# Retention in halves of 64 tokens, all its small products in 64x64 quarters of the array, the decay factor on the token rows

## The chip, the cores and the metric

The kernel runs on one core of one Trainium2 chip. The metric is device time in microseconds (us) of that core. Three timed runs of the kernel before gave 444.48, 444.49 and 444.55; the median is 444.49.

A core has a matrix engine (PE in the profile; PEld is its loading of weights), a vector engine (DVE), an engine for activations and copies (ACT), a general engine that also issues gathers and scatters (POOL), and SP, which in this kernel issues nearly all loads. DMA engines move data between the chip's main memory and on-chip memory. A matrix product reads both operands from on-chip memory and writes a *bank* of an accumulator memory, of which there are eight; DVE and ACT copy from there.

## What is computed

```python
state = gamma * state + einsum('bhd,bhe->bhde', k[:, :, t], v[:, :, t])   # for t in 768 tokens
y[:, :, t] = scale * einsum('bhd,bhde->bhe', q[:, :, t], state)
...
x = y, as 3072 rows of 512 (4 batches x 768 tokens; 8 heads x 64)
logits = x @ w_gate + modality_bias[modality_id]
e = argmax(logits);  gate = softmax(logits)[e]
out = gate * (relu(x @ w1[e]) @ w2[e])             # 8 experts, w1 512x1024, w2 1024x512
```

All of it is float32. The first two lines are *retention* (attention with a decaying state), the rest a mixture of experts in which each token goes to one expert.

## The kernel before

**Retention** goes through 24 chunks of 128 tokens (`NN`; six to each of four batches). The heads stand in four groups `g` of two heads `j`, so that a group's features fill 128 partitions. For a chunk, PE makes four kinds of products, each eight of them, all in float32:

- `scores` (L190): keys by queries of the chunk, 64 features deep, 128 by 128 tokens out, one bank for each `j`. DVE multiplies them by a triangular mask into `a` (L195).
- `state` (L251): keys by the decayed values `vd`, added in one bank `st` over a batch's six chunks. ACT copies it to `s` (L256) for the next chunk. The last chunk of a batch needs none.
- `heads_out`: the earlier chunks' part, `s` by queries (L211, absent in a batch's first chunk), and the chunk's own, `vd` by `a` (L217), added into two banks. DVE multiplies the sum by a decay factor for each feature and token into `yT` (L223, four instructions of 128x128).
- `tokens_out` (L234): `yT` is turned to token rows `x` and multiplied by the gate weights in the same four products, 136 columns wide. ACT copies the rows to `xs` (L238), and DVE adds up the gate logits (L242).

POOL makes `vd`, values times a decay factor (`decay_v`, L827). Queries and keys by feature (`kq`, 512 KB a chunk) and keys and values by token (`kv`, 512 KB) are loaded by SP. For every three chunks a *group* is routed: DVE finds expert and gate, PE makes ranks (`rk`, L299 to L306), POOL scatters the rows `xs` to `x_dram`, sorted by expert. After some groups (`EVENTS`) a list of full slots of 256 rows of one expert is made, by small products `pc`, `pk` and `pt` and DVE operations that end in `lst` (L512).

**Experts** are done in 12 jobs of 256 rows. `start_job` lets SP read expert and rows from a list; SP then loads the expert's `w1` (`raw1`, four times 512 KB), the rows (`xg`) and `w2` (`raw2`). Each piece of weights is cut into a high and a low part, `hi` by ACT (L596) and `lo` by DVE (L598), and PE makes three products for each exact one: `h_e` (L652) and `o_e` (L667). Rows beyond the jobs go in small units at the end.

**The order** on PE, ACT, DVE and SP is written out by the program: these engines work their instructions off in the order of the calls. Retention is a generator that yields twice for each chunk. First it runs alone (the *dense stage*), until `2 * (DENSE - n)` half steps after the first list has been issued at chunk `n` (`DENSE = 10`). After that, each job of 16 steps takes in five half steps of retention (the *job stage*). SP's loads are one queue: what a chunk or a job needs stands behind what was called earlier. `kv` has three buffers, and four more for chunks 3 to 6; an accumulator bank is handed on when its last reader is done.

## Time and profile before

| what | value |
|---|---|
| median of three runs | 444.49 us |
| the profiled execution's own time | 446.39 us |
| its span, first to last instruction | 444.4 us |
| mean granted PE clock | 0.976 |
| PE busy | 414.1 us, 93% of the span |
| PEld, DVE, ACT, POOL busy | 358.7, 265.5, 185.7, 103.9 us |
| first product of the first job (`h_e`) | 66.2 us |
| last retention product | about 264 us |
| last product of PE | 433.5 us |

The profile is one execution. A row of a group gives the source line, the engine, the operation, what it writes and reads, its shapes and count; then the busy time and the mean of one in ns; then the idle time of the engine before it and what ended it. The chain of waits is the work that ended last, followed back in time. A float32 product of the program shows as two MATMUL records and two LDWEIGHTS records, so that a row "x16" of retention is eight products. A table by stretch of time gives, for each stretch, its length, the busy time and the number of records of each engine, the granted clock of PE (1.00 is full), the share of time that the DMA engines were busy, and GB/s.

### The profile page before, as it was taken

The page shows a single profiled execution, that of the slowest core. Times are in us where ns is not written, and L with a number is a line of the kernel's source. Part 1 is how long each engine was busy: PE and PEld are TensorE (multiplying, and loading weights), DVE is VectorE, ACT ScalarE, POOL GpSimd, SP SyncE. Part 2 cuts the span into 40 slices and gives each one's busy share as a digit, 9 for nine tenths or more (in the row PEclk, how much of TensorE's full clock was granted, in tenths as well). Part 3 has the DMA queues.
Part 4 walks back from the last instruction along what each step waited for, and adds up shares of the span by engine and source line. Part 5 has one row for each costly group of instructions (what it writes and reads, how often), then busy time and mean ns, then how long its engine had stood idle before and what let it go on. Part 6 is the DMA issues. An engine that isn't in the chain of part 4 may idle for free.

```text
span 444.4 us, 9973 instructions
## 1 busy us (share of the span) xinstructions
PE 414.1 (93%) x3619; PEld 358.7 (81%) x3619; DVE 265.5 (60%) x619; ACT 185.7 (42%) x323; POOL 103.9 (23%) x130
## 2 busy tenths in 40 slices
PE   2997898998999999999999999999999999999990
PEld 2886788987988978987987897989789898868860
DVE  1697479846646765695576667855556473725500
ACT  1222143634426334634544453545455655536310
POOL 2225306012401131142112303068410101001010
PEclk9999598999999999999999999999999999999996
DMA  8992697980542758334950405445167579995000
GB/s 279 400 406 104 222 380 274 350 333 28 169 145 96 250 194 324 119 125 154 288 180 26 150 1 175 140 150 215 45 227 280 190 257 337 412 386 195 1 25 19
DMA packets 28722, 89.45 MB, mean 201 GB/s; under 512 B 5310, under 2 KB 5438, under 8 KB 28672
## 3 DMA queue, kind: packets, MB, share of 16 engines
q1 hardware_dynamic: 23200, 74.27, 47.4%
q0 software_dynamic: 5184, 14.10, 8.3%
q8 instruction: 29, 0.48, 0.5%
q10 hardware_dynamic: 288, 0.43, 0.3%
q14 instruction: 21, 0.17, 0.1%
HBM read 91.19 MB, written 17.84 MB: 245 GB/s over the span
## 4 chain that ended last, share of the span: by engine, by line
PE 56%; issue 20%; DVE 8%; DMA 6%; POOL 5%; ACT 2%; SPq 0%; POOLq 0%; ACTq 0%; DVEq 0%
PE h_e L652 17%; PE o_e L667 16%; PE sc L190 6%; PE x L234 5%; PE y L217 5%; PE y L211 3%; POOL x_dram L388 2%; DVE lo_e L598 2%; PE st L251 2%; DMA x_dram<-zer,pad_i 2%; POOL out_dram L680 2%; ACT hi_e L596 2%; DMA kq<-in_qkv_dram 1%; DMA raw<-in_w_dram 1%; PE xp_e L637 1%
## 5 line engine op out<-in xcount | busy, mean ns | idle before, releaser
L598 DVE TENSOR_TENSOR lo_e<-raw,hi_e 128x1024 fp32r<-128x1024 f32 x80 | 98.1, 1226 | 65.4 <-ACT hi_e L596 59.6
L652 PE MATMUL h_e<-xTh,lo_e 128*128 128x256 f32 x320 | 91.3, 285 | 1.7 <-DVE lo_e L598 1.7
L652 PE MATMUL h_e<-xTh,hi_e 128*128 128x256 f32 x320 | 92.8, 290 | 0.0
L652 PE MATMUL h_e<-xTl,hi_e 128*128 128x256 f32 x320 | 91.1, 285 | 0.0
L596 ACT CAST hi_e<-raw 128x1024 fp32r<-128x1024 f32 x80 | 83.4, 1043 | 0.0
L667 PE MATMUL o_e<-hi_e,hTh 128*128 128x512 f32 x160 | 65.8, 411 | 0.0
L652 PEld LDWEIGHTS h_e<-xTh,hi_e 128*128 128x128 f32 x320 | 61.9, 193 | 3.1 <-issue 1.0
L652 PEld LDWEIGHTS h_e<-xTh,lo_e 128*128 128x128 f32 x320 | 62.0, 194 | 2.2 <-DVE lo_e L598 1.9
L667 PE MATMUL o_e<-lo_e,hTh 128*128 128x512 f32 x160 | 62.7, 392 | 0.5 <-DVE lo_e L598 0.5
L667 PE MATMUL o_e<-hi_e,hTl 128*128 128x512 f32 x160 | 62.6, 391 | 0.0
L652 PEld LDWEIGHTS h_e<-xTl,hi_e 128*128 128x128 f32 x320 | 62.0, 194 | 0.0
L605 ACT ACTIVATE hTh<-h_e 128x256 fp32r<-128x256 f32 x80 | 30.7, 383 | 60.4 <-PE h_e L652 56.5
L827 POOL TENSOR_TENSOR vd<-kv,cst 128x512 f32<-128x512 f32 x24 | 25.6, 1068 | 108.0 <-PE y L217 58.6
L195 DVE TENSOR_TENSOR a<-sc,cst 128x512 f32<-128x512 f32 x48 | 30.8, 683 | 24.3 <-PE sc L190 24.3
L680 POOL DMA_INDIRECT out_dram<-o_e,xg_e x20 | 19.9, 994 | 107.9 <-ACT o_e L679 83.9
L606 DVE SCALAR_TENSOR_TENSOR hTl<-h_e,hTh 128x256 fp32r<-128x256 f32 x80 | 33.3, 418 | 16.2 <-ACT hTh L605 14.0
L679 ACT ACTIVATE o_e<-o_e,xg_e 128x512 f32<-128x512 f32 x20 | 13.8, 688 | 67.2 <-issue 35.5
L190 PE MATMUL sc<-kq 64*128 64x128 f32 x384 | 30.6, 304 | 7.9 <-DMA kq<-in_qkv_dram 7.9
L328 POOL DMA_INDIRECT x_dram<-xs,pos x24 | 28.8, 1201 | 33.2 <-DVE key L469 18.4
L667 PEld LDWEIGHTS o_e<-lo_e,hTh 128*128 128x128 f32 x160 | 30.0, 188 | 7.7 <-DVE lo_e L598 1.0
L667 PEld LDWEIGHTS o_e<-hi_e,hTh 128*128 128x128 f32 x160 | 30.1, 188 | 7.5 <-issue 1.4
L667 PEld LDWEIGHTS o_e<-hi_e,hTl 128*128 128x128 f32 x160 | 30.1, 188 | 5.1
(167 smaller groups left out, 604.9 us busy)
## 6 DMA issues: line engine op xcount, KB each, us to landing
raw<-in_w_dram SPq DMA_DIRECT2D x96, 512.0 KB
kv<-in_qkv_dram SPq DMA_DIRECT2D x24, 512.0 KB
kq<-in_qkv_dram SPq DMA_DIRECT2D x23, 512.0 KB
xg_e<-x_dram SPq DMA_DIRECT2D x20, 272.0 KB
wa_u<-in_w_dram SPq DMA_DIRECT2D x8, 512.0 KB
wb_u<-in_w_dram SPq DMA_DIRECT2D x8, 512.0 KB
xg_s<-x_dram SPq DMA_DIRECT2D x4, 272.0 KB
x_dram<-xs,pos POOLq DMA_INDIRECT x24
```

The costliest lines, as they stand in the source:

```text
L190: nc.tensor.matmul(pe[j][:, g * P : (g + 1) * P], kt[r, g], qt[r, g], start=True, stop=True, skip_group_check=True,)
L195: nc.vector.tensor_tensor(a[:, j], pe[j].rearrange("p (h t) -> p h t", t=P), mask.unsqueeze(1).to_broadcast([P, NG, P]), op=ALU.mult,)
L217: nc.tensor.matmul(py[j][g % 2 * D : (g % 2 + 1) * D, g // 2], vd[:, 2 * g + j], a[:, j, g], start=(s is None and g < 2), stop=(g >= 2), s ...
L328: ins = nc.gpsimd.indirect_dma_start(out=x_dram[:, :], out_offset=bass.IndirectOffsetOnAxis(ap=pos[:, i : i + 1], axis=0), in_=xs.rearrang ...
L596: nc.scalar.copy(hi, raws[m][i])
L598: nc.vector.tensor_tensor(lo, raws[m][i], hi.bitcast(F32), op=ALU.subtract)
L605: nc.scalar.activation(hi, src, AF.Relu)
L606: nc.vector.scalar_tensor_tensor(lo, src, 0.0, hi.bitcast(F32), op0=ALU.max, op1=ALU.subtract)
L652: nc.tensor.matmul(ph, s["w1"][f // 2][wi][:, o : o + P], s["xT"][kc // 2][a][:, kc % 2, :], start=(n == 0), stop=(n == 3 * KC - 1),)
L667: nc.tensor.matmul(po, hT[f][a][:, hh * P : (hh + 1) * P], s["w2"][f // 2][wi][:, (f % 2) * DM : (f % 2 + 1) * DM], start=(n == 0), stop=( ...
L680: ins = nc.gpsimd.indirect_dma_start(out=out[:, :], out_offset=bass.IndirectOffsetOnAxis(ap=xg.bitcast(I32)[:, 0, P : P + 1], axis=0), in_ ...
L827: ins = nc.gpsimd.tensor_tensor(vds[n], vv, dec[:, n % NCH].unsqueeze(2).to_broadcast([P, H, D]), op=ALU.mult)
```

## The change

Each chunk is worked in two halves `u` of 64 tokens, and every product of retention but `tokens_out` becomes 64x64x64: it uses a quarter of the 128x128 array, given by the half of the partitions it reads (`low` or `high`) and the half it writes. `scores` within a half, the part between the halves through a state of its own, and so on: 64 quarter products for a chunk, 56 where a chunk is a batch's first or last. `run` issues two of the `low` half, then two of the `high` half, and so on. `quarters(n)` is one stretch of them on PE: scores of chunk n+1, the state after chunk n and after the first half of chunk n+1, the rest of the output of chunk n-1 and most of that of chunk n.

```diff
-DENSE = 10
+DENSE = 12
-ROW = DM // P * (P + NE)
+ROW = DM + 2
+XW = P + 2 * NE
...
+    def keep_state(n, u):
+        s = sts[n, u] = wk.tile([P, NG, D], F32, tag="s", name=f"s{u}_{n}", bufs=3)
+        b = (n - 1 + u) // NCH
+        nc.scalar.copy(s, pst.pop(b) if u and n % NCH == NCH - 1 else pst[b])
+
+    def run(low, high):
+        for i in range(0, max(len(low), len(high)), 2):
+            for out_, l, r, start in low[i : i + 2] + high[i : i + 2]:
+                nc.tensor.matmul(out_, l, r, start=start, stop=True, skip_group_check=True)
+
+    def quarters(n):
+        more = 0 <= n < NN and (n + 1) % NCH
+        ...
+        if n + 1 < NN:
+            low += scores(n + 1, 0)
+        if more:
+            high += grown(n, 1)
+        if n > 0:
+            low += inner(n - 1, 1, 0)
+            high += inner(n - 1, 0, 1)
+        if 0 <= n < NN:
+            low += inner(n, 0, 0, start=True) + outer(n, 0)
+            high += inner(n, 1, 1, start=True) + outer(n, 1)
+        run(low, high)
+        if more:
+            keep_state(n + 1, 0)
+        if n + 1 < NN:
+            run(grown(n + 1, 0), scores(n + 1, 1))
+            keep_state(n + 1, 1)
...
-        for b in range(NG):
-            nc.vector.scalar_tensor_tensor(
-                yT[:, b], py[b // 2][:, b % 2], step[:, n % NCH, b : b + 1], dcq[:, b],
-                op0=ALU.mult, op1=ALU.mult,
-            )
+    def y_out(n):
+        yT = wk.tile([P, NG, P], F32, tag="yT", name=f"yT_{n}")
+        for j in range(2):
+            nc.scalar.copy(yT[:, 2 * j : 2 * j + 2], py[n][j])
...
-            nc.scalar.copy(xs[:, 2 * u : 2 * u + 2], px)
+            gained(lh[:, hs], px[:, :, P:], NE)
+            if u == 0:
+                gained(x, px[:, :, :P], D)
+            else:
+                for i in range(4):
+                    nc.scalar.activation(
+                        x[:, i], px[:, i // 2, rows(i % 2)], AF.Copy,
+                        scale=gain[:, c, 4 * u + i : 4 * u + i + 1],
+                    )
...
-        vds[n] = wk.tile([P, H, D], F32, tag="vd", name=f"vd_{n}", bufs=2)
+        vds[n] = wk.tile([P, H, D], F32, tag="vd", name=f"vd_{n}", bufs=3)
...
+        for n in range(NN + 1):
+            if n > 0:
+                if n > 1:
+                    tokens_out(n - 2, yT)
+                if n > 1 and (n - 1) % GRP == 0:
+                    route((n - 1) // GRP - 1)
+                yield n
+            quarters(n)
+            if n + 1 < NN:
+                masked(n + 1)
+            if n + 2 < NN:
+                decay_v(n + 2)
+            if n > 0:
+                yT = y_out(n - 1)
+            load_kv(n + 7 if n < 3 else n + 3)
+            load_kq(n + 8 if n < 4 else n + 4)
```

`grown` is the state's products (into the bank `st`), `inner` the output within a half and between the halves, `outer` the earlier state's part, `masked` DVE's mask (two instructions of 128x256 in place of 128x512). `gained` multiplies the token rows by the decay factor, on DVE for the gate logits `lh` and for the first half of the row; ACT does the other half in four instructions of 128x64. The gate weights double to 16 columns a group, so that `tokens_out` writes 144 columns. A row of `x_dram` shrinks from 272 KB to 257 KB for 128 rows, the table `decq` (256 KB) is no longer loaded, and the constants grow from 168 to 212 KB and stand behind the first `kq` on ACT's queue. In the small units `w2` is loaded in eight pieces in place of four. All products of retention have line L257, `tokens_out` L313, the state's copy L251, the `yT` copies L302, and the row's scaling on ACT L335.

Three places of the order follow. On PE, the kernel before had these rows shortly ahead of the first `h_e` of job 0 (only `rk` and `pc` stand between; `xp1` are the rows of job 0 turned, `e10` is that job; `kv_10` is chunk 10's, and chunk 11's `kv` was first used inside job 0):

```order
L637 MATMUL xp1_e10_962<-cst_76,xg0_e10_798 128x128
L637 MATMUL xp1_e10_962<-cst_76,xg1_e10_800 128x128
L251 MATMUL st_6_580<-vd_10_868,kv_10_683 64x64 x8
L190 MATMUL sc0_11_990<-kq_11_422 128x128
L190 MATMUL sc1_11_991<-kq_11_422 128x128
```

The change has, also between the first list (`pt1`) and the first `h_e`, the whole of `quarters(10)`; this is where its second `run` begins (`s1_10` is the state inside chunk 10, `sc1_11` the scores of the second half of chunk 11):

```order
L257 MATMUL y0_10_1337<-kq_10_431,s1_10_1284 64x64 x2
L257 MATMUL y1_10_1338<-kq_10_431,s1_10_1284 64x64 x2
L257 MATMUL st_6_767<-vd_11_1289,kv_11_1194 64x64 x2
L257 MATMUL sc1_11_1390<-kq_11_541 64x64 x2
L257 MATMUL st_6_767<-vd_11_1289,kv_11_1194 64x64 x2
```

So `kv_11` and `vd_11` are now needed in the dense stage, and `tokens_out` of chunks 9 and 10, `quarters(11)`, the rows of job 0 turned (`xp`) and `quarters(12)` stand between this and the first `h_e`.

SP's queue of loads has, in the change, this order there; it is that of the kernel before, where line numbers and the size of `xg` differ (`raw10` to `raw13`, the pieces of `w1`, and `xg0` stand ahead of these rows; `ISA` rows are waits):

```order
L705 DMA xg1_e10_1108<-x_dram_75 128x514
L677 ISA
L677 DMA raw20_107<-in_w2_dram 128x1024
L677 ISA
L677 DMA raw21_108<-in_w2_dram 128x1024
L677 ISA
L677 DMA raw22_109<-in_w2_dram 128x1024
L677 ISA
L677 DMA raw23_110<-in_w2_dram 128x1024
L108 DMA kv_11_1194<-in_qkv_dram 128x1024
```

So `kv_11` stands behind the whole first set of weights in both kernels; only what waits for it has moved.

On ACT, a chunk of the dense stage was this before (the state's copy, then the rows):

```order
L256 COPY s_8_816<-st_6_580 128x256
L238 COPY xs_7_833<-x_7_0_834 128x272
L238 COPY xs_7_833<-x_7_1_838 128x272
L256 COPY s_9_878<-st_6_580 128x256
L238 COPY xs_8_895<-x_8_0_896 128x272
L238 COPY xs_8_895<-x_8_1_900 128x272
```

and is this in the change:

```order
L335 ACTIVATE xs_6_1089<-x_6_1_1096,cst_76 128x64 x4
L251 COPY s0_9_1165<-st_6_767 128x256
L251 COPY s1_9_1184<-st_6_767 128x256
L302 COPY yT_7_1191<-y0_7_941 128x256
L302 COPY yT_7_1191<-y1_7_942 128x256
L335 ACTIVATE xs_7_1198<-x_7_1_1205,cst_76 128x64 x4
```

The copy to `s0_9` reads the bank that the last eight products of state in the same stretch then write again; `yT` has moved from DVE to ACT, behind both copies of the state.

236 lines of the change are left out of this document (124 added, 112 removed).

## Prediction

> **What bounds the kernel now.** I read the page's busy times first, then a table by stretch of time, the chain of waits, and the timeline between the first list and the first job.
>
> ```profile
> PE 414.1 (93%) x3619; PEld 358.7 (81%) x3619; DVE 265.5 (60%) x619; ACT 185.7 (42%) x323; POOL 103.9 (23%) x130
> PEclk9999598999999999999999999999999999999996
> ```
>
> ```profile
> 13.40:44.10 30.70, 27.34 (x443) 23.82 (x439) 25.74 (x95) 6.81 (x19) 11.72 (x18) 1.00 0.76 301
> 44.10:54.40 10.30, 8.60 (x81) 7.49 (x77) 5.18 (x22) 1.14 (x3) 3.52 (x4) 0.50 0.55 202
> 66.20:264.60 198.40, 194.73 (x1789) 171.26 (x1790) 132.84 (x312) 88.85 (x160) 45.58 (x57) 0.99 0.52 180
> 264.60:433.50 168.90, 166.27 (x1090) 141.25 (x1088) 92.43 (x163) 82.04 (x129) 37.29 (x35) 1.00 0.56 200
> ```
>
> PE is the bound. In the job stage (66.2 to 264.6, where jobs and retention run together) it is busy 194.73 of 198.40 us, so there PE's time is the time. In the dense stage it is busy 27.34 of 30.70, and then runs 10.3 us at half clock (0.50). ACT is busy 88.85 of 198.40 (45%) in the job stage: not the bound, but not idle either.
>
> **What a quarter product costs.** This is what retention takes from PE in the job stage, by line, and how single groups follow one another in the chain (start, length, what).
>
> ```profile
> 66.17:264.60 198.43, 13.95 (x192) 11.65 (x192) 0.99 0.52 180
> 66.17:264.60 198.43, 6.86 (x160) 5.47 (x160) 0.99 0.52 180
> 66.17:264.60 198.43, 8.01 (x192) 5.11 (x192) 0.99 0.52 180
> 66.17:264.60 198.43, 15.32 (x224) 11.94 (x224) 0.99 0.52 180
> 66.17:264.60 198.43, 16.45 (x120) 15.34 (x120) 0.99 0.52 180
> ```
>
> (scores L190, state L251, heads_out L211 and L217, tokens_out L234, in this order.)
>
> ```profile
> 115.36 0.93 PE x L234 x8
> 116.30 0.60 PE y L211 x16
> 116.89 1.02 PE y L217 x16
> 122.41 0.62 PE st L251 x16
> 123.02 1.09 PE sc L190 x16
> ```
>
> A group of scores, state or heads_out is 16 records, two at a time: 8 steps. State streams 64 columns, scores 128. The 64 columns more cost 1.09 - 0.62 = 0.47 over 8 steps, so 64 columns cost 0.0588 a step and 0.62 - 0.47 = 0.15 is start-up. In the change every step streams 64 columns, and four records (four quarters) can share one. That four do share is told by one merged row:
>
> ```profile
> 144.57 0.34 PE L211 MATMUL y<-kq,s 64*64 64x128 f32 x4
> 48.47 0.21 PE L508 MATMUL pt<-ohs,vals 96*1 96x2 bf16 x3 [1.70 <-DVE ohs L494]
> L508 PE MATMUL pt<-ohs,vals 96*1 96x2 bf16 x15 | 1.1, 164 | 1.7 <-DVE ohs L494 1.7
> ```
>
> Four L211 records, two in each row half, take 0.34 together. A whole stretch (64 products, 128 records, 32 steps) then takes 0.15 + 32 x 0.0588 = 2.03. `tokens_out`, 144 columns for 136, takes 0.93 x 144/136 = 0.985.
>
> **Job stage, gain.** By records over group size there are 12 groups of scores, 10 of state, 12 of L211, 14 of L217 and 15 of L234: 12 x 1.09 + 10 x 0.62 + 12 x 0.60 + 14 x 1.02 + 15 x 0.93 = 54.7 us. The change, which moves some chunks' work ahead of the first job, has there 12 stretches with 656 products (328 steps) and 13 `tokens_out`: 328 x 0.0588 + 12 x 0.15 + 13 x 0.985 = 33.9. **Gain 20.8.**
>
> By the Trainium skill, "TensorE: Matmul & The Clock Gate", section "Wait — 56ns, not 53.3ns?", start to start never drops below about 25 ns however small the product. No row here has a steady stream so small. 1312 records at that spacing would be an estimate of 32.8 us in place of 19.3, and the stage would gain 7 in place of 21.
>
> **Job stage, a new wait.** Inside a stretch the second `run` starts with products into the state's bank, and ACT's copy `s0` must have read that bank first; the copy waits for the first `run`. So PE waits for ACT in the middle of its own stretch. Before, the copy lay beside other PE work.
>
> ```profile
> 123.12 0.37 ACT L256 COPY s<-st 128x256 f32<-128x256 f32 x1 [0.30 <-PE st L251]
> L596 ACT CAST hi_e<-raw 128x1024 fp32r<-128x1024 f32 x47 | 49.0, 1043 | 0.0
> L605 ACT ACTIVATE hTh<-h_e 128x256 fp32r<-128x256 f32 x48 | 18.4, 382 | 41.6 <-PE h_e L652 40.0
> L238 ACT COPY xs<-x 128x272 f32<-128x272 f32 x30 | 11.1, 388 | 12.5 <-issue 10.8 <-PE x L234 0.9
> L610 ACT CAST xTh<-xp_e 128x512 fp32r<-128x512 f32 x10 | 5.4, 590 | 1.8 <-PE xp_e L637 1.8
> L256 ACT COPY s<-st 128x256 f32<-128x256 f32 x11 | 4.1, 374 | 8.9 <-PE st L251 8.8
> L271 ACT ACTIVATE ex<-lg 128x24 f32<-128x24 f32 x4 | 0.9, 223 | 7.5 <-DVE lg L269 7.5
> ```
>
> The state's products ended at 123.03 and the copy began at 123.12: a hand-off of 0.09. With ACT free the wait is 0.374 + 2 x 0.09 = 0.55. ACT works in order, and casts take 49.0 of 198.4 us of it: one time in four it is inside a cast of 1.043, half of it left, which adds 0.13. The `hTh` (0.382) of the `h_e` that ended before the stretch has the first `run` (0.15 + 24 x 0.0588 = 1.56) as cover. Twelve stretches at 0.68: **loss 8.2**. At best the wait is partly bubbles that PE had anyway: 0; at worst the cast has always just begun: 12 x (0.55 + 1.04) = 19. I take 8.2, since cast and copy both have rows. Behind the waiting product all of PE is queued, the next `h_e` too. **Job stage net: -12.6.**
>
> "TensorEngine Tiling (Array Packing)" of the Trainium skill, section "PSUM Bottleneck", warns that tiling speeds up TensorE but not the emptying of its banks, so that the copy may become the bottleneck. By count of the rows above it does not bind as throughput: ACT has for a chunk two copies of 0.374, two of `yT` of 0.388 and four row pieces of at most 0.223, together 2.42, against a chunk of 4.5 in the dense stage. It binds as the latency just costed.
>
> **Dense stage.** These are chain pieces and the routing's list.
>
> ```profile
> 14.72 1.09 PE sc L190 x16
> 19.02 1.14 PE sc L190 x16
> 38.26 1.14 PE x L234 x8
> 68.26 4.40 PE h_e L652 x23
> 97.39 0.87 PE xp_e L637 x8
> ```
>
> ```profile
> 48.72 0.15 DVE L512 TENSOR_TENSOR lst<-pt,base_e 1x6 int32<-1x6 f32 x1
> 51.33 1.95 SPq L590 DMA_DIRECT2D raw<-in_w_dram  x4
> 53.54 0.86 SPq L618 DMA_DIRECT2D xg_e<-x_dram  x2
> 58.64 0.34 SPq L107 DMA_DIRECT2D kv<-in_qkv_dram  x1
> 69.35 1.04 POOL L827 TENSOR_TENSOR vd<-kv,cst 128x512 f32<-128x512 f32 x1 [9.81 <-DMA kv<-in_qkv_dram]
> ```
>
> Before, a chunk took 19.02 - 14.72 = 4.30. After: the stretch 2.03, its wait for `s0` 0.55, `tokens_out` 0.985, and ahead of it a wait for `yT`, which ACT copies after the stretch and behind `s1`: 0.374 + 0.388 + 2 x 0.09 = 0.94. Sum 4.5. So although PE's products are cheaper, a chunk isn't faster: PE works and ACT copies in turn. The first `tokens_out` comes some 2 us later (17.9, for a stretch and two waits replace a group each of state and scores), and five chunks later `x_5` ends at 17.9 + 5 x 4.5 + 0.985 = 41.4; before it ended at 38.26 + 1.14 = 39.4. The routing's `ex` on ACT then stands behind a state and a `yT` copy, about 0.8 more. I put the first list 3 us later: 48.87 + 3 = 51.9.
>
> **The load that is now waited for.** `kv` of chunk 11 is issued behind the job's first weights. Before, POOL started `vd_11` at 69.35, 20.48 after the list, having waited 9.81 for that load; no PE work ahead of the first job needed it. In the change `quarters(10)` needs it, in the dense stage. PE gets there after three `tokens_out`, two stretches, a first `run` and two pairs of waits: 3 x 0.985 + 2 x 2.03 + 1.56 + 2 x 1.49 = 11.6 after the list, at 63.5. The data comes at 51.9 + 20.48 + 1.04 (`vd`) + 0.09 = 73.5. **PE stands for 10 us.** After that: second `run` 0.47, ten small products at 0.07 (0.21 for three) 0.7, `x_9` 0.985, `quarters(11)` 1.8 (28 steps), `yT` 0.94, `x_10` 0.985, `xp` 0.87, `quarters(12)` 1.8, and its `s0` behind casts of `xTh` (0.59) and `hi`, 0.55 + 1.2: in all 10.3. The first full run of `h_e` starts at 83.8; before at 68.26. **Loss 15.5.** If the queue in the new kernel lets `kv_11` land 5 us sooner, the loss is 10; if weights come later too, 18.
>
> **Clock.** What 10 us of a standing PE do is seen twice before:
>
> ```profile
> 40.71:44.12 3.41, 1.20 (x22) 0.99 (x22) 3.18 (x15) 0.22 (x1) 2.27 (x5) 1.00 0.42 167
> 64.60:68.00 3.40, 1.81 (x23) 1.27 (x19) 3.21 (x12) 2.74 (x5) 0.00 (x0) 1.00 1.03 404
> ```
>
> A window of 3.4 us with PE busy 1.20 of it was followed by the half clock, until 54.4; PE had resumed at about 48.6, so 5.8 us of work ran at half speed, half of that lost. The same after the new stall: **loss 2.9** (0 if the short products after it count as busy soon; 5.8 if twice as long).
>
> **Off the path.** One DVE row stands for the relief:
>
> ```profile
> L223 DVE SCALAR_TENSOR_TENSOR yT<-y,cst,dcq 128x128 f32<-128x128 f32 x96 | 27.0, 342 | 7.8 <-PE y L217 7.8
> ```
>
> DVE loses four of these a chunk and gains the scaling of half a row and of the logits; it waits for PE before and after (7.8 idle here), so I give nothing. The smaller row, the absent table, the constants moved on ACT's queue and four loads more in each of the two small units (8 x 0.34 = 2.7 if nothing covered them) lie beside 168.9 us in which PE has no gap: nothing.
>
> **Sum.** The profiled span is 444.4, the median of the runs 444.49 (the execution's own time, 446.39, is 2 us above both; I keep to the median). 444.5 - 12.6 + 15.5 + 2.9 = 450.3. **Forecast 450.**
>
> **Rivals.**
> - *Faster, 439.* ACT is ready when the stretches need it (3 in place of 8.2), the clock stays up (0 for 2.9) and the list isn't later (0 for 3): 450.3 - 11.1 = 439. For it: PE had 3.7 us of gaps in the job stage already, and ACT is idle 55%. Against it: `kv_11` alone keeps 12.5 us, and the dense chain PE, ACT, PE has no other work to hide in. Chance 0.27.
> - *The quarters don't share: 473.* If records start no faster than the three `pt` products (0.21 - 0.164 = 0.046 for two, 23 ns each), a stretch of 128 takes 2.94: job stage 12 x 0.9 = 10.8 more, about 8 more in the dense stage ahead of the list and after the stall, and 3 of waits. If only two of four share, 656 steps come to 53.2 with `tokens_out`, as much as before, and the end is about the same 473. Against it: the x4 row. The point from which it decides is a stretch of over 2.5 us. Chance 0.13.
> - *The change does only what it says of work, and the stall is hidden (432).* That takes a `kv_11` that is there by 63.5, which SP's order excludes; I count it into the first.
>
> **How the numbers follow.** The forecast case has 0.60, and reaches by its own bounds from 443 (waits of the job stage near 2) to 460 (waits at 19). The range that holds 8 in 10 is 437 to 467: it leaves out the far end of each rival. A measurement of this kernel tells no change within 0.2%, that is 443.6 to 445.4; 0.07 of the chance lies there, taken from the forecast's low end and the fast rival's high end. So faster 0.27, the same 0.07, slower 0.66.
>
> **What would show it.** A stretch (L257) with about 128 records of 2.0 to 2.2 us, and 2.9 or more for the second rival. At 62 to 74 us PE's wait of about 10 us for `vd` from POOL, and POOL's for the load of `kv`; the first `h_e` at about 84. Under PE's waits in the job stage, state products released by ACT's `s0`, some 0.7 each. PEclk below 9 after 73. The forecast is wrong if the first `h_e` starts before 76, or if from there to PE's last product it takes more than 365.2 (433.5 - 68.26) less 8.

## The result, and the profile after

| | before | predicted | after |
|---|---|---|---|
| median | 444.49 us | 450.0 (437 to 467) | 465.6 us (464.2 to 466.0, 4 runs) |
| ratio to before | | | 1.0469, 95% interval 1.0446 to 1.0492 |
| profiled span | 444.4 | 450.3 | 464.1 |
| first list | 48.9 | 51.9 | 54.8 |
| first full run of `h_e` | 68.3 | 83.8 | 90.1 |
| from there to PE's last product | 365.2 | 352.6 + 2.9 | 362.9 |

Ratios here and below leave out executions that took over 1.5% more than the fastest of the same kernel, among them one of 748.86 us and one of 1307.25 us further down.

The change is slower, as forecast, but by 21 us where 5.5 were forecast. By the spans, 6.3 us of the difference to the forecast lie ahead of the first full run of `h_e`, and 7.4 behind it: the job stage was to become 10 to 13 us shorter, and became 2.3 shorter.

The page of the kernel after, its busy times and PE's granted clock in 40 slices:

```profile
PE 406.0 (87%) x5155; PEld 356.9 (77%) x5155; DVE 246.0 (53%) x595; ACT 211.3 (46%) x453; POOL 102.1 (22%) x130
PEclk9899886998997999999999989997999999999996
```

PE has 8 us less to do (414.1 before) and is a smaller share of a longer span. The clock shows low slices all through the job stage (a 7 at the 13th slice, an 8 at the 24th, a 7 at the 28th), where before had one place only, at the 5th to 7th.

The job stage as one stretch, before and after (columns as in the prediction's tables by stretch):

```profile
68.26:433.49 365.23, 360.63 (x2876) 312.35 (x2876) 223.21 (x471) 169.75 (x286) 82.87 (x92) 1.00 0.54 188
```

```profile
90.07:452.98 362.91, 348.44 (x3422) 305.30 (x3416) 206.99 (x436) 181.97 (x351) 73.63 (x82) 0.97 0.51 176
```

PE's busy time fell by 12.2 us, the stage by 2.3: 9.9 us came back as idle time of PE (4.6 to 14.5). And the busy time itself should have fallen by some 19: the same stretch for the job's own products, `o_e` alone, before and after:

```profile
68.26:433.49 365.23, 143.09 (x576) 104.65 (x576) 1.00 0.54 188
```

```profile
90.07:452.98 362.91, 148.11 (x576) 108.66 (x576) 0.97 0.51 176
```

576 products that the change does not touch take 5.0 us more, since parts of them run at half clock. Counted from each product's start to the next one's, retention's small products fell from 40.8 to 25.1 us and `tokens_out` from 15.2 to 11.6: 19.3 in all, of the 20.8 predicted. So **the gain on PE is there, and is taken back by idle time (9.9) and by the clock (about 7)**: 19.3 - 9.9 - 7.1 = 2.3.

PE's waits in the whole kernel after (who waited for whom: us in total, times, longest):

```profile
PE st L257 <- POOL vd L918: 9.8, 3, 6.6
PE x L313 <- ACT yT L302: 5.5, 8, 0.8
...
PE y L257 <- issue: 4.3, 4, 2.2
PE st L257 <- issue: 4.2, 3, 3.5
PE rk L386 <- DVE oh L367: 4.0, 3, 1.9
PE xp_e L724 <- DMA xg_e<-x_dram: 2.9, 2, 2.8
PE pc L546 <- DVE crep L541: 2.6, 4, 0.7
...
PE sc L257 <- issue: 2.0, 2, 1.6
```

The first line holds the load of `kv_11` (6.6), the second is the `yT` wait; both were in the prediction. The "issue" lines (10.5 us) are waits for which the profile names no releaser. They turn out to be two different things.

**Most of them: PE has no instructions.** In the dense stage of the kernel after:

```profile
26.41 0.34 PE L257 MATMUL y<-a,vd 64*64 64x64 f32 x9
28.93 0.28 PE L257 MATMUL y<-a,vd 64*64 64x64 f32 x4 [2.18 <-issue]
```

PE stops in the middle of a run of like products, and no instruction of another engine ends in the 0.35 us before it goes on. The trace's DMA packets have a queue of kind "instruction" (q8) whose packets, 16,384 bytes each, go with PE's count: 29 packets for 7,238 products and weight loads before, 41 for 10,310 after, so some 250 for each. A stretch's 128 records and their 128 weight loads are about one packet's worth. These packets, and the gaps inside stretches that the profile puts down to "issue" and that don't end with a copy of ACT:

```
packet begins, lands   PE idle from .. to   from landing to PE's next product
13.82  14.93           15.23 .. 16.39       1.46
20.15  21.26           22.14 .. 22.62       1.36
26.48  27.57           26.75 .. 28.93       1.36
31.04  32.06           33.08 .. 33.57       1.51
64.38  65.36           65.19 .. 66.76       1.40
81.04  82.82           83.85 .. 84.33       1.51
```

Each gap ends 1.36 to 1.51 us after a packet lands. From the packet's begin to PE's next product it is 2.4 to 2.6 us in five of the six, and a stretch uses up a packet's worth in 2.02. The six gaps are 6.4 us. Ahead of three of them some instruction of another engine ends within 0.3 us too, ahead of the other three none does. In the experiments' kernels such gaps of over 0.5 us also end 1.2 to 1.5 us after a landing, with one exception (0.94 us at 57.9 in a_dense10, 0.2 us after). In some the gap begins before its packet does.

**The others: ACT's copy `s0`**, the new wait of the prediction. The longest, at the first stretch inside a job, on PE and then on ACT:

```profile
103.77 0.37 PE L257 MATMUL st<-vd,kv 64*64 64x64 f32 x2 [3.51 <-issue]
```

```profile
101.97 0.22 ACT L358 ACTIVATE ex<-lg 128x24 f32<-128x24 f32 x1 [2.66 <-DVE lg L356]
102.09 0.37 ACT L692 ACTIVATE hTh<-h_e 128x256 fp32r<-128x256 f32 x1
102.36 1.03 ACT L683 CAST hi_e<-raw 128x1024 fp32r<-128x1024 f32 x1
103.29 0.38 ACT L251 COPY s<-st 128x256 f32<-128x256 f32 x1
```

The product goes on 0.10 us after the copy's end (103.67). Ahead of the copy on ACT stand a routing's `ex`, for which ACT itself waited 2.66 us for DVE, then `hTh`, then a cast. Three more gaps end 0.09 to 0.10 us after such a copy (0.23, 0.46 and 1.31 us; the last is put down to `vd` by the waits above, which had been done for 5 us): 5.5 us in all, 4.0 of them in the job stage. (The gap of 1.31 also ends 1.45 us after a packet's landing; in a_yT the same gap ends 0.10 us after the copy and 2.3 us after a landing, so the copy is the likelier cause.) Of the twelve stretches there, ten show no wait for it.

**Where the clock falls.** PE's busy time (second number, after the length) in the 3.41 us ahead of each half-clock stretch of the job stage:

```profile
100.15:103.56 3.41, 0.10 (x8) 0.00 (x0) 3.10 (x15) 1.59 (x4) 1.54 (x4) 1.00 0.73 207
141.11:144.52 3.41, 1.92 (x61) 1.57 (x61) 3.10 (x17) 1.71 (x4) 0.00 (x0) 1.00 0.00 0
226.44:229.85 3.41, 1.63 (x69) 1.32 (x72) 3.31 (x12) 1.47 (x3) 0.00 (x0) 1.00 0.30 121
267.40:270.81 3.41, 1.41 (x14) 1.08 (x13) 3.10 (x17) 1.71 (x4) 0.00 (x0) 1.00 0.51 160
311.77:315.18 3.41, 0.94 (x5) 0.41 (x3) 1.23 (x1) 1.25 (x2) 2.75 (x3) 1.00 0.45 124
```

One is the `s0` wait above, three are routings (PE waits for `oh`, then `crep`, while DVE is busy 3.1 to 3.3 of 3.41), the last is the wait for `xg`. 23.9 us of the job stage then run at half clock, against 3.2 before.

### The profile page after: what moved, and what is told of

Same layout as the page of the kernel before. It is cut to its first block, busy times and chain, and to the rows that moved or that the text cites. A ratio compares the mean times of both kernels' runs of the same rounds, so it can differ in the third digit from the quotient of the medians.

```text
span 464.1 us, 13180 instructions
## 1 busy us (share of the span) xinstructions
PE 406.0 (87%) x5155; PEld 356.9 (77%) x5155; DVE 246.0 (53%) x595; ACT 211.3 (46%) x453; POOL 102.1 (22%) x130
## 4 chain that ended last, share of the span: by engine, by line
PE 34%; issue 18%; DVE 6%; DMA 4%; ACT 3%; POOL 3%; SPq 0%; POOLq 0%; ACTq 0%
PE o_e L754 14%; PE h_e L739 14%; DVE lo_e L685 3%; ACT hi_e L683 2%; PE x L313 2%; PE y L257 2%; DMA x_dram<-zer,pad_i 1%; POOL out_dram L767 1%; DMA raw<-in_w_dram 1%; PE xp_e L724 1%; POOL x_dram L475 1%; PE sc L257 1%; DMA wa_u<-in_w_dram 1%; DVE hTl L693 1%; DMA xg_e<-x_dram 1%
## 5 line engine op out<-in xcount | busy, mean ns | idle before, releaser
L683 ACT CAST hi_e<-raw 128x1024 fp32r<-128x1024 f32 x80 | 83.8, 1047 | 0.0
L754 PE MATMUL o_e<-hi_e,hTh 128*128 128x512 f32 x160 | 68.0, 425 | 0.0
L754 PE MATMUL o_e<-hi_e,hTl 128*128 128x512 f32 x160 | 64.6, 404 | 0.0
L918 POOL TENSOR_TENSOR vd<-kv,cst 128x512 f32<-128x512 f32 x24 | 28.1, 1174 | 116.6 <-PE y L257 82.2
L257 PE MATMUL st<-vd,kv 64*64 64x64 f32 x704 | 34.9, 246 | 14.7 <-POOL vd L918 9.8
L335 ACT ACTIVATE xs<-x,cst 128x64 f32<-128x64 f32 x96 | 22.3, 315 | 52.0 <-issue 34.9
L257 PE MATMUL sc<-kq 64*64 64x64 f32 x768 | 38.9, 248 | 7.7 <-DMA kq<-in_qkv_dram 5.2
L251 ACT COPY s<-st 128x256 f32<-128x256 f32 x44 | 16.5, 375 | 59.5 <-PE sc L257 36.8
L257 PEld LDWEIGHTS st<-vd,kv 64*64 64x64 f32 x704 | 29.2, 156 | 16.3 <-POOL vd L918 10.2
L208 DVE TENSOR_TENSOR a<-sc,cst 128x256 f32<-128x256 f32 x48 | 19.5, 419 | 41.8 <-PE sc L257 31.1
L257 PEld LDWEIGHTS sc<-kq 64*64 64x64 f32 x768 | 32.1, 157 | 11.5 <-DMA kq<-in_qkv_dram 5.2
```

The costliest lines, as they stand in the source:

```text
L208: nc.vector.tensor_tensor(att[n][:, j], psc.pop((n, j)), half.unsqueeze(1).to_broadcast([P, NG, D]), op=ALU.mult,)
L251: nc.scalar.copy(s, pst.pop(b) if u and n % NCH == NCH - 1 else pst[b])
L257: nc.tensor.matmul(out_, l, r, start=start, stop=True, skip_group_check=True)
L335: nc.scalar.activation(x[:, i], px[:, i // 2, rows(i % 2)], AF.Copy, scale=gain[:, c, 4 * u + i : 4 * u + i + 1],)
L683: nc.scalar.copy(hi, raws[m][i])
L754: nc.tensor.matmul(po, hT[f][a][:, hh * P : (hh + 1) * P], s["w2"][f // 2][wi][:, (f % 2) * DM : (f % 2 + 1) * DM], start=(n == 0), stop=( ...
```

## The experiments

Theory after the result: the dense stage loses by the supply of instructions and by PE and ACT working in turn; the job stage loses what PE gains by waits that PE's work used to cover, and by the clock behind them. Rivals: the two chunks more ahead of the first job (DENSE) or `kv_11` alone; ACT's new work; or no gain of the quarters at all.

The experiments ran on several chips. On each the kernel before was timed beside them, and the ratios are to these runs: its median there was 443.1 to 443.4 us (444.5 beside the change), and 448.9 on one chip that is named below. Small differences between experiments are therefore read from the ratios.

### How many chunks stand ahead of the first job

`DENSE = 12` back to 10 in the kernel after, and 12 in place of 10 in the kernel before.

> The changed kernel with DENSE = 10 in place of 12: two chunks fewer ahead of the first job. Theory (the load of kv_11 and the two chunks behind it cost what the dense stage lost): PE's stand of 6.6 us for vd_11 is gone from the dense stage, the first h_e comes at 70 to 74 in place of 90.1, the job stage takes two chunks more (2 x (2.02 + 0.985) = 6.0 us), so some 452 in place of 465.6. Rival (the job stage is where it is lost, by PE standing for instructions and by half-clock windows, and more chunks there make more of them): 458 or more, with three or more issue gaps of over 1 us after the first h_e.

> The kernel before with DENSE = 12: two chunks more ahead of the first job. Theory (the longer dense stage meets the load of kv_11 in the old structure too): PE waits for vd_11, the first h_e at about 79 in place of 68.3, the job stage two chunks shorter (2 x 4.26 = 8.5), the time about 447. Rival (the wait comes of the new order of products alone): first h_e at 68.3 + 8.5 = 77 with no wait of over 2 us, the time 444 to 445.

| | time | ratio to before | first `h_e` | job stage | PE idle there | half clock there |
|---|---|---|---|---|---|---|
| before | 444.5 | 1 | 68.3 | 365.2 | 4.6 | 3.2 |
| before, DENSE 12 | 452.2 | 1.0157 (1.0092 to 1.0221) | 81.4 | 362.4 | 8.4 | 10.2 |
| after, DENSE 10 | 456.8 | 1.0295 (1.0252 to 1.0338) | 79.3 | 364.9 | 13.2 | 14.0 |
| after | 465.6 | 1.0469 (1.0446 to 1.0492) | 90.1 | 362.9 | 14.5 | 23.9 |

(The first `h_e` is counted from where its wait for `lo_e`, if it has one, is over. The stages of the second row are of an execution of 456.57 us, 4.3 over its median.) By the ratios DENSE costs 1.7% in the change and 1.6% in the kernel before, some 7 to 8 us in either, so rather over a third of the loss is this one number. Not for the reason given: in the change the first `h_e` comes at 79 and not at 70 to 74, because PE still stands 5.1 us for `vd_11`, now inside job 0 (72.5 to 77.6), and the time lies between what theory and rival said. In the kernel before PE waits 3.0 us for a `kq` (68.8 to 71.8) and not for `vd_11`.

In the execution shown, the old structure, with 8.5 us of retention less in the job stage, gains 2.8 there, and the rest is idle time and half clock, as in the change. That this is no matter of quarters is not shown by it: the granted clock of this execution was 0.967, that of the other three 0.976 to 0.979, which over their length is, as an estimate, 8 to 11 us less of half clock.

### The load of kv_11

```diff
                 if 1 not in job:
+                    load_kv(11)
+                    load_kq(12)
                     rows_in(job)
```

> The changed kernel with kv_11 and kq_12 loaded ahead of the rows xg and of w2 of job 0; the order of everything else is as it was. Theory (PE stands for that load alone): PE's wait for vd_11 falls from 6.6 us to under 1, at most 2 of it come back at kv_12, the first h_e at 84 to 85 in place of 90.1, the time about 460. Rival (instructions or the clock take the place of the wait): h_e no earlier than 88, the time 464 or more.

463.59 (1.0432, 1.0397 to 1.0467), 2 us less than the change, which the intervals don't tell from nothing. `vd_11` now starts at 69.1 (75.0 before this edit), and PE's wait for it falls from 6.6 to 2.0, but the chain behind it has 1.7 more at `kv_12`, an issue gap of 1.4 in the routing, and a longer half clock (23.9 us ahead of the first job, 20.5 without the edit). The first `h_e` comes at 87.6, 2.5 us sooner. The rival is nearer: the wait is real, and most of it is covered again by the next late thing.

### More instructions, and slower ones

In the kernel before, scores and heads_out in products of 64 columns:

```diff
-            for j in range(2):
...
+            for u in range(2):
+                for j in range(2):
...
-                    pe[j][:, g * P : (g + 1) * P], kt[r, g], qt[r, g],
...
+                        pe[j][:, g * P + u * D : g * P + (u + 1) * D], kt[r, g], qt[r, g, w],
```

> The kernel before with each product of scores and heads_out cut into two of 64 columns: the same quarters and halves of the array as before, twice the instructions there, the same columns streamed. Theory (PE's instructions come in blocks of 256, and a stretch that uses up a block in 2 us stands until the next one lands): idle PE with no releaser (issue) of 0.4 us and more appears in the dense stage, where before there was none, 2 to 5 us in all; the time 446 to 450. Rival (the issue gaps of the changed kernel have another cause, such as quarters or banks): no such gaps, groups as long as before, 444 to 445.

470.35 (1.0586, 1.0556 to 1.0617): both wrong in the time. There is no issue gap of 0.35 us or more, as the rival has it, with 120 records a chunk in the dense stage, so the number of instructions alone does not stop PE; they also come at a slower pace here than in a stretch. The time is lost in scores. The chain of this kernel:

```profile
67.48 1.93 PE sc L192 x32
70.53 0.67 PE y L215 x30
71.20 1.08 PE y L222 x32
```

`y` L222 has its records doubled and halved, and takes 1.08 (1.02 before); L215, whose 64x64 products can share the array four at a time, 0.67 with 30 records (0.60 with 16). But scores take 1.93 with 32 records, where 16 took 1.09: their weights are still 128 wide, and with that a pair of records of 64 columns takes 0.112 us (starts 7 and 105 ns apart in turn), nearly what a pair of 128 columns takes (0.136). Counted from start to start in the whole kernel, scores take 52.3 us for 29.1: 23 of the 26.9 us lost. So this run changes two things, and says little of what more instructions alone would cost.

In the kernel after, one product of 424 columns into an unused bank after every eight quarter products:

```diff
...
+            if i % 4 == 2:
+                nc.tensor.matmul(pw[:, :C_END], ident, cst, start=True, stop=True)
```

> The changed kernel with one product of 424 columns into an unused bank after every eight quarter products, read by nobody: 144 records a stretch in place of 128, and 2.02 + 2.9 = 4.9 us for them. Theory (a stretch uses up a block of 256 instructions faster than the next lands): with more instructions, but slower ones, the issue gaps (10.5 us in all, longest 3.5) fall to under 1.5 us. Rival (the gaps have to do with the number of instructions, or with what the quarters write): gaps of 0.5 us and more stay in number and size. The time itself says nothing: 24 x 2.9 = 70 us of work added, some 525 to 535.

618.2: the added product takes 0.8 us, not 0.36, and the sum is 152 us. PE's waits of this kernel name no issue gap at all, with more instructions than in the change. That fits both halves of the explanation above (the next packet lands in time, and ACT's copy is done), and speaks against a cause in the number of instructions or in what the quarters write. Which gap is which is told by the landing times, not by this run.

### The yT copies

`y_out` called between the two runs of a stretch:

```diff
             keep_state(n + 1, 0)
+        yT = y_out(n - 1) if n > 0 else None
         if n + 1 < NN:
             run(grown(n + 1, 0), scores(n + 1, 1))
...
-            if n > 0:
-                yT = y_out(n - 1)
```

> The changed kernel with ACT's two yT copies of a chunk called between the two runs of a stretch, ahead of the copy s1 (what they read is complete after the first run). Theory (in the dense stage PE waits for the yT copy behind s1, 0.71 to 0.79 us a chunk, 8 times): these waits fall to 0.4 or less, the list comes 2 to 3 us sooner (54.8 before), the time falls by 2 to 4 us to about 462. Rival (the dense stage is held by the supply of instructions, so a wait that goes comes back as an issue gap): the sum of issue gaps ahead of the first job grows by as much, the list at 54 or later, 465.

461.09 (1.0420, 1.0385 to 1.0455). That is 4.5 us less than the change, but its chip was faster by 1: by the ratios it is 2 us less, and 3.6 less than a second measurement of the change further down (1.0501). The eight waits of 0.3 to 0.8 are gone, the list comes 2.6 us sooner (52.2), and some of it comes back: the four early supply gaps sum to 7.5 us in place of 4.3. Theory and rival hold side by side, and the gain is barely clear of the noise.

### The routing's waits and the clock

An empty tick between the routing's DVE part and its products; and products into an unused bank ahead of `rk` and `pc`:

```diff
-            todo.extend([a, b, c])
+            todo.extend([a, lambda: None, b, c])
```

```diff
...
+        warm(gr, 3)
         pr = bank(f"rk_{gr}")[:, : GRP * NE].rearrange("p (c e) -> p c e", e=NE)
```

> The changed kernel with an empty tick between the DVE part of a routing and its products rk and pc on PE, from the second list on (the first is as it was): PE reaches rk two steps of a job later. Theory (with less retention work on PE, it reaches the routing ahead of DVE, and the 3.4 us windows with such waits in them are followed by half clock): the waits for oh, crep and what follows at 141 to 145, 225 to 230 and 268 to 271 (6.4 us in all) go, and with them three of the half-clock stretches after the first h_e (13.7 us at half speed, 6.8 lost); the job stage 350 to 355 in place of 362.9, the time 453 to 458. Rival (the job stage is held by something else, since in four kernels it took 363 to 365 whatever work was in it): it stays within 2 us of 362.9, the time 464 to 467.

> The changed kernel with products into an unused bank ahead of rk (three of 424 columns, some 1.1 us) and pc (two, some 0.7 us) of the routings from the fourth on; they depend on nothing and their sums are read by nobody. PE then does not stand while DVE is late. Theory (the clock falls because PE stands there): the half-clock stretches at 144 to 151, 230 to 233 and 271 to 274 are gone, 6.8 us less, at most 3 us of the products not hidden by the waits: 459 to 463. Rival (the clock falls for another cause): the half clock stays and the time rises by 1 to 4 us, to 467 to 469.

a_warm: 471.32 (1.0611, 1.0535 to 1.0688). The time went up, since each of these products takes 0.8 us and not 0.36; small products take 17 us more of PE in the job stage. The clock is told all the same. The job stage from 140 to 240 and from 240 to 300, with the products and without them:

```profile
140.00:240.00 100.00, 97.89 (x1371) 82.90 (x1370) 60.94 (x165) 48.43 (x114) 21.10 (x29) 1.00 0.45 152
240.00:300.00 60.00, 58.82 (x448) 51.02 (x447) 38.33 (x103) 30.24 (x61) 10.67 (x15) 1.00 0.35 122
```

```profile
140.00:240.00 100.00, 93.98 (x1346) 82.40 (x1345) 60.13 (x166) 50.20 (x116) 24.95 (x33) 0.95 0.48 163
240.00:300.00 60.00, 58.00 (x451) 52.26 (x450) 39.42 (x102) 31.16 (x61) 13.37 (x15) 0.97 0.38 127
```

All three half-clock stretches behind routings are gone (granted clock 1.00 for 0.95 and 0.97). So it is PE standing there that lets the clock fall.

a_tick: 465.94 (1.0511, 1.0454 to 1.0568), no gain. The waits for `oh` and `crep` behind the first list are gone, and half clock falls from 23.9 to 13.7 us, the job stage from 362.9 to 360.3; but the first `h_e` came 2.0 us later, and new waits stand further on: 1.5 us at 163 for a bank that DVE's `lst` releases, 0.9 and 1.0 for `dg`, and a second one for `xg`, of 1.4; idle time of the job stage is 16.0 us for 14.5. In this kernel the edit is undecided; it comes back below.

### ACT's work

In the job stage of the change ACT stands 33.6 us ahead of its row pieces, by the theory mostly because they read the bank that DVE reads for the logits (the profile names DVE's `lh` for 8.6 us, and no releaser for 25.0):

```profile
L335 ACT ACTIVATE xs<-x,cst 128x64 f32<-128x64 f32 x52 | 12.1, 316 | 33.6 <-issue 25.0 <-DVE lh L321 8.6
```

(before: 12.5 ahead of the rows' copy, in the prediction's rows). All rows scaled by DVE:

> The changed kernel with both halves of a chunk's token rows scaled by DVE; ACT's four pieces are gone. Theory (the pieces read the bank that DVE reads for the logits, ACT waits for DVE behind a cut lo of 1.23 us, and hTh, hTl and the routing behind it are late; ACT stands 33.6 us ahead of these pieces in the job stage, where it stood 12.5 ahead of the rows' copy before): that idle time goes, PE's waits after the first h_e fall by 4 us or more, the job stage from 362.9 to 354 to 358, the time to 456 to 461. Rival (DVE gets 0.42 us a chunk more and is later at the routing): the job stage 362 to 365, the time 464 to 468.

> The changed kernel once more, as it is, beside the two runs after it on one chip, since on the chip of the last four runs the kernel before itself spread from 443.65 to 453.34. Theory and rival alike: 464 to 467; another time than that says how much of a difference between chips is to be allowed.

> The edit of a_dve once more (all rows scaled by DVE), beside the changed kernel on the same chip. Theory (477 there was that chip, where stretches stood for instructions in pieces of 0.4 us; the edit frees ACT): 2 to 8 under after_2. Rival (DVE is later at everything): 2 to 10 over after_2.

The first of these gave 477.0 on a chip where the kernel before itself ran from 443.65 to 453.34, and where one stretch of it got its instructions in pieces of about ten every 0.74 us; so it was run again beside the change. There: the change 464.49 (1.0501, 1.0451 to 1.0551), the edit 463.39 (1.0444, 1.0397 to 1.0491). The intervals overlap. What ACT's row pieces cost can't be told from nothing; this theory falls. The change, measured for a second time, is as slow as the first time.

### Together

> The changed kernel with DENSE = 10, the yT copies between the two runs, and all rows scaled by DVE. Theory (the causes are separate): alone they gave -8.8, -4.5 and what the run beside this one gives; with some 5 for that, 445 to 450. Rival (they share one cause, PE's stand in the dense stage for instructions): the second adds nothing, 452 to 456.

> As the run before this, and the stretch in two: the first run (96 records) is one half step, the second run (32 records) and the rows of the chunk are the other, so that between them a job's products stand in the job stage; the dense stage has the same sequence as before. Theory (a burst of 256 instructions in 2 us outruns their supply): no issue gap of over 0.4 us after the first h_e (3.5, 1.3 and 0.5 in the changed kernel), 2 to 4 us under c_dve_yT_10. Rival (these gaps are of the first job's loads, not of the burst): they stay, and the time is within 1 us of c_dve_yT_10.

> As c_split, with kv_11 loaded ahead of the rows and w2 of job 0. Theory (kv_11 is what PE stands for at the first job): PE's wait for it (5.1 us with DENSE = 10) falls under 1 and the time by 3 to 5 against c_split. Rival (w2 or the clock takes its place, as at DENSE = 12, where 2 of 6.6 us were won): 0 to 2 less.

On the same chip as the first a_dve: 450.22 (1.0084, 1.0036 to 1.0131), 475.23 (1.0617, 1.0527 to 1.0707) and 475.18 (1.0632, 1.0520 to 1.0743). The first is about the sum of what its parts gave alone, by the times (465.6 - 8.8 - 4.5 = 452) and more than the sum by the ratios. It fits separate causes for DENSE and `yT`, but with this chip's spread of the kernel before it doesn't exclude the rival (452 to 456) by much. Cutting the stretch in two half steps took away the waits for `s0` behind the first `h_e` (0.87 and 0.17 us in the first of these runs), as told, and cost 25 us elsewhere. New "issue" gaps of up to 0.8 us stand in the job's own products at 325 to 338 (3.5 us in all), between two packets that begin at 309 and 341. PE waits 2.2 and 1.8 us for ACT's `fence` copies, half clock in the job stage goes from 4.7 to 23.9 us and the stage from 357.1 to 377.9. Why the job's own products fell behind there is left open. In c_split_kv, with the same job stage, PE's longest wait for `vd` is 3.1 us (3.2 without the edit), so the load could not be priced: the rival (0 to 2 less) is nearer.

### Old products in the dense stage, quarters in the job stage

If the gain on PE is real and the dense stage and the waits take it back, then quarters belong where jobs fill the gaps. Chunk 12 begins a batch, so that its state starts from nothing: chunks 0 to 11 go in the products of the kernel before, 12 to 23 in stretches.

```diff
-DENSE = 12
+DENSE = 10
+SW = 12
...
+        for n in range(SW):
...
+            nxt = state_o(n) if (n + 1) % NCH else None
...
+                nex = scores_o(n + 1)
...
+            yield n
...
+                tokens_out(*prev)
...
+            prev = (n, heads_o(n, cur, s))
...
+            yield n
...
+        for n in range(SW, NN + 1):
...
+                tokens_out(n - 2, yT)
...
+                yield n
+            yT = quarters(n)
...
             yield n
```

`state_o`, `scores_o` and `heads_o` are the products of the kernel before, in its order; for `n = 11` there are no such scores, but the parts of `quarters(11)` that belong to chunk 12. The second loop has the order of the change. Rows are scaled by DVE, and `yT` is copied by ACT, in the later chunks between the two runs.

> Retention in two ways: chunks 0 to 11 with the products of the kernel before (a state bank of their own, 128 by 128 masks), chunks 12 to 23 in stretches of quarters, and DENSE = 10; rows scaled by DVE, yT copied by ACT, between the two runs in the later chunks. The dense stage has only products of the first kind, and of the second kind none is used ahead of the first job. Theory (quarters win on PE where jobs fill the waits, and lose in the dense stage, by the supply of instructions and by ACT's copies in turn with PE): list at 49 to 51, first h_e at 67 to 71, no issue gap of over 0.4 us ahead of it, job stage 12 x (3.33 - 2.02) = 15.7 us shorter on PE, of which half comes back as waits (as in c_dve_yT_10, 357.1 against 365.2), so 434 to 439. Rival (the job stage takes 363 to 365 whatever is in it): 443 to 446.

> As h12, with the change from old products to stretches at chunk 6 in place of 12 (the second batch): chunks 6 to 10 are then stretches in the dense stage, and all else is h12. Theory (in the dense stage a stretch costs more than the old products, since its instructions come too late and ACT's copies stand between PE's runs): issue gaps of 0.4 us and more come back ahead of the first job, 2 to 4 us in all, and PE stands for vd_11 in the first job or ahead of it; the first h_e at 71 to 76 in place of 66.5, the time 442 to 450 against 438.8. Rival (only the first chunks, with all loads of the start under way, are late): h_e at 66 to 68, 436 to 440.

> As h12, with the empty tick of a_tick between the DVE part of a routing and its products on PE. Theory (in the job stage PE comes to rk and pc ahead of DVE): its waits for oh and crep after the first h_e (0.49, 0.67, 0.51, 0.69 and 0.63 behind them) go, 2 to 3 us less, 436 to 437. Rival (the routing is a chain, and what is called later is waited for later, as a_tick gave nothing): 438 to 440.

> As h12, with the sixteen scatters of padding rows after the last list called in four ticks in place of eight. They end at 308.2, and the load of the next rows (issued at 310.5) stands behind them, for which PE waits 2.2 us at 311 to 314, followed by 3.4 us of half clock. Theory (it is the ticks that space them): they end at 298 to 302, that wait and that half clock go, 3 to 4 us less, 434.5 to 436. Rival (POOL itself is the limit, 16 x 1.3 us): they end where they did, 438 to 440.

| | time | ratio to before | first list | first `h_e` | job stage | idle there |
|---|---|---|---|---|---|---|
| before | 443.1 | 1 | 48.9 | 68.3 | 365.2 | 4.6 |
| h12 | 438.78 | 0.9893 (0.9861 to 0.9926) | 49.6 | 67.9 | 358.2 | 9.3 |
| h6 | 443.58 | 1.0003 (0.9974 to 1.0031) | 44.8 | 74.0 | 353.8 | 9.7 |
| h12_tick | 433.91 | 0.9787 (0.9754 to 0.9820) | 49.2 | 67.6 | 354.9 | 8.0 |
| h12_pad | 436.84 | 0.9869 (0.9847 to 0.9891) | 49.7 | 66.9 | 355.5 | 8.2 |

(The time before is that of these runs' chips, 443.12 and 443.05; the profile of before is the one shown above. The first `h_e` is counted as in the first table.)

**h12 beats both kernels**, the one before by 1.1%, as the theory has it: with old products the dense stage has no issue gap of 0.4 us or more, list and first `h_e` come about when they did before, and the job stage is 7.0 us shorter, about the 7 to 8 told. Of the 13.7 us less of retention work in it (28.6 + 13.7 for 40.8 + 15.2), 4.7 come back as idle time. From c_dve_yT_10 (450.2, first list 57.1, first `h_e` 79.0, job stage 357.1) h12 differs only by the old products of chunks 0 to 11, with their buffers, and by its chip. The job stage is about as long in both, so what these products win lies in the dense stage.

h6 differs from h12 in one number, and loses 4.8 by the medians. The execution shown took 440.71, and its span is only 1.5 us over that of h12; what the slower ones lose besides no trace shows. Its list comes 4.8 us sooner, so a stretch with less DMA under way does not lose (231 GB/s from 26 to 44 us; the change, with its four gaps, had 378 from 10 to 35); but behind the list, while 4 MB of weights are loaded, PE has a gap of 2.07 us that ends 1.35 us after a packet, and stands for the loads that the faster work reaches sooner:

```profile
PE st L313 <- POOL vd L969: 6.9, 2, 3.8
...
PE st L313 <- issue: 2.6, 3, 2.1
```

So stretches in the dense stage do cost time, but the theory told for h6 holds behind the list alone, and there the loads that come late weigh more (6.9 us) than the instructions (2.1).

**h12_tick is the best: 2.1% under the kernel before (1.8 to 2.5).** What gave nothing in the change gives 4.9 us here by the medians, and 3.8 by the spans of the profiles. PE's job stages of h12 and of h12_tick:

```profile
67.87:426.08 358.21, 348.94 (x3644) 305.24 (x3644) 217.50 (x475) 172.45 (x302) 81.56 (x92) 1.00 0.56 191
```

```profile
67.60:422.50 354.90, 346.92 (x3650) 304.44 (x3650) 219.51 (x475) 172.37 (x302) 82.73 (x92) 1.00 0.56 193
```

1.3 us less idle and 2.0 less busy, of which 1.7 is the half clock that h12 has at 314 to 318 and this kernel has not. The waits for `oh` and `crep` after the first `h_e` are gone, as told (3.2 us), but 1.6 us more for `ohs` and 1.0 more for ACT's `s` come in their place. The half clock goes by where the wait for `xg` falls, as the next run shows, so that part is not shown to be the tick's.

h12_pad moved the padding by nothing that matters: the last scatter begins where it did (308.2, then 306.1 with the first one 2.1 sooner too), so the ticks don't space them, and PE waits for `xg` as before, 1.85 and 0.35 us. Its median is 2 us lower all the same, within the intervals of the two, and its profile has 6.8 us less of half clock. The 3.41 us windows around this wait in h12, then in h12_pad:

```profile
307.47:310.88 3.41, 3.41 (x16) 2.78 (x15) 0.00 (x0) 0.83 (x2) 1.40 (x2) 1.00 0.02 0
310.88:314.29 3.41, 1.17 (x7) 0.54 (x6) 1.22 (x1) 0.79 (x1) 0.98 (x1) 1.00 0.69 231
```

```profile
306.99:310.40 3.41, 2.31 (x10) 1.51 (x9) 0.76 (x1) 1.62 (x2) 1.10 (x2) 1.00 0.26 66
310.40:313.81 3.41, 2.32 (x14) 1.92 (x15) 1.26 (x3) 1.41 (x3) 0.00 (x0) 1.00 0.43 166
```

In h12 the wait lies in one window (busy 1.17) and half clock follows; in h12_pad it lies across two (2.31 and 2.32), and none does. In h12_tick it lies across two as well (2.10 and 2.55).

## Why the prediction was right and wrong

- **What a quarter product costs: right.** Stretches without a wait take 2.02 us (2.03 predicted), and `tokens_out` 0.98. The gain of 20.8 measures 19.3. One reading behind it was loose: that scores differ from state by their columns. In b_split scores of 64 columns with weights still 128 wide were hardly faster; the change halves both, so that the price came out right without this being known.
- **The job stage's new wait: the right mechanism, twice too large.** 8.2 was predicted over twelve stretches; it is 4.0, in two. The step that failed is "the copy waits for the first run". The products that the copy waits for are in the first third of it, and the 0.94 us of steps behind them cover the 0.55. The wait shows only where ACT is behind a routing's `ex` or a cast. By luck this error brought the forecast 4 us nearer.
- **The job stage's other waits: missing, and this is the main error.** The step that failed is "Job stage net: -12.6". It took the new work out of PE's time, added one wait, and left all other times as they were, since before PE had few gaps. But what PE waits for at a routing (DVE, 0.6 to 1.3 us each for `oh` and `crep`) and at `xg` (2.8) does not shrink with PE's work. About 6 us of idle time come from there: 14.5, less 4.6 that were there before, less 4.0 for `s0`. With the clock behind these waits the net is 19.3 - 4.0 - 5.9 - 7.1 = 2.3.
- **The clock: one step where there are five.** 2.9 us were counted once, behind the first stall. Each wait, or row of short waits, that leaves too little of a 3.41 us window busy brings 3.4 us of half clock or more; 20 us more of them in the job stage cost about 7 on top of what the first stall cost. In the kept traces, from 12 us on, every full-clock window with PE busy for less than 1.59 us was followed by half clock, none with more than 2.28 was, and between the two it went either way.
- **The dense stage: +15.5 predicted, +21.8 measured.** A chunk's sum of 4.5 holds where no supply gap falls (`tokens_out` at 36.4, 40.5 and 45.1, 4.1 and 4.6 apart) and not where one does (6.4, 6.5 and 5.5 apart at the start; half clock from 18.2 to 21.6 and a routing's products lie in there too). No term was there for PE's instructions: four gaps, 4.3 us, ahead of the list, which came 2.9 us later than predicted, and two, 2.0 us, behind it. Half clock added to both sides of the list: 20.5 us of it lie ahead of the first `h_e`, 10.2 before. `kv_11` came as told, 21.4 us after the list to the end of `vd_11` (21.6), and PE stood 6.6 us for it, not 10, being late itself:

```profile
75.03 1.04 POOL L918 TENSOR_TENSOR vd<-kv,cst 128x512 f32<-128x512 f32 x1 [17.27 <-DMA kv<-in_qkv_dram]
```

- **The rivals.** *Faster* failed in two of its three conditions (clock, list). *The quarters don't share* is refuted by 2.02. The rule of some 25 ns from start to start (the Trainium skill, "TensorE: Matmul & The Clock Gate", section "Wait — 56ns, not 53.3ns?") does not hold for quarters here: 128 records in 2.02 us are 15.8 ns each. The Trainium skill's warning that emptying the banks may become the bottleneck ("TensorEngine Tiling (Array Packing)", section "PSUM Bottleneck") does hold, as a latency: the `yT` copies cost 5.5 us of waits, and hiding them gave some 2 to 4. (ACT's row pieces take 0.316 us each and not "at most 0.223", which leaves the reading on throughput as it was: ACT is busy 46% of the span.)
- Of what was to show it: the stretch's length and the wait for `vd` are there, the first `h_e` came 6 us later than said, and the sign that the forecast would be wrong (the stage less than 8 us shorter) came true.

## What to carry to other kernels

A matrix product that becomes cheaper in a stage that PE bounds uncovers what PE's time had covered: list the waits that hang on other engines there, at their fixed length, before the gain is booked, and add the half clock that follows where they empty much of a window. Put a new, denser form where other PE work can fill its gaps (here the job stage), and keep the old form where it cannot. Where a run of small products uses up 256 instructions in about 2 us, their supply is a term of the sum.

## What the runs showed of the hardware that was not expected

- PE's instructions come in packets of 16 KB, and at 128 records in 2.02 us PE stands: it goes on 1.2 to 1.5 us after a packet's landing, about 2.5 us after its begin. The Trainium skill, "Runtime: NRT & Kernel Launch", section "Instruction fetch mechanics", tells of blocks of 256 instructions, which agrees with the packets' size, and calls their cost mostly hidden; here six of them cost 6.4 us.
- In b_split 32 records of 64 columns with 128-wide weights took 1.93 us, nearly twice the 1.08 us of 32 records with 64-wide weights (L222), and 16 records of 128 columns took 1.09. That the spacing goes by the wider of columns and weights would explain it; only this one case was run.
- The half clock goes by fixed windows of 3.41 us: in the change it begins at 103.56, 144.52, 229.85, 270.81 and 315.18, which are 12, 25, 12 and 13 such windows apart. The same wait of 2.2 us brought it where it lay in one window, with PE busy 1.17 of 3.41, and not where it lay across two, with 2.31 and 2.32.
